# Issuing two sets of small tiled matmuls of neighbouring steps as one alternating run, in a fused recurrence and MLP kernel

## The chip, the cores and the metric

The kernel runs on one core of a Trainium2 chip. The metric is the device time of one execution in microseconds (us); several runs are given by their median. The engines are named as the profile names them: PE (TensorE, the matrix engine; PEld is its weight loads), DVE (VectorE), ACT (ScalarE), POOL (GpSimd) and SP, whose queue issues the loads and stores here. Lines such as L819 are lines of the kernel before.

## The reference

A recurrence over 768 tokens is followed by an MLP. Everything is float32.

```python
# q, k, v: (4, 8, 768, 48), beta: (4, 8, 768)
k_n = k / (norm(k, axis=-1) + 1e-06)
state = zeros((B, H, D, D))
for t in range(S):
    y[:, :, t] = einsum('bhd,bhde->bhe', q[:, :, t], state)
    v_old = einsum('bhde,bhd->bhe', state, k_n[:, :, t])
    state = state + beta[:, :, t, None, None] * einsum('bhd,bhe->bhde', k_n[:, :, t], v[:, :, t] - v_old)
x = y.transpose(0, 2, 1, 3).reshape(B * S, H * D)     # 3072 x 384
h = x @ w_in                                          # 384 x 2048
g = h * clip(h + 3.0, 0.0, 6.0) / 6.0
out = g @ w_out                                       # 2048 x 384
```

## The kernel before

**The recurrence in chunks.** Tokens are taken in 24 steps t of C = 32 tokens. The 128 partitions hold 4 batches of 32 tokens; rows(b) is the stretch of batch b. Inside a chunk the recurrence is solved by a triangular inverse, so a step is a few small matmuls:

- *prep* (L497) makes what does not depend on the state: the scaled keys kb on POOL (L502), transposes pt on PE (L516), KQ on ACT (L524), the products sc of keys and queries on PE (L539), and on DVE the masked L and LB (L550). The mask mb is beta times a triangle of ones, one part positive and one negative (L478, two POOL operations of 128x256 in each step). bkb (L490, POOL) is beta times the keys.
- *inverse* (L738) inverts the triangles of four steps at once on DVE: some sixty operations pr (L751) and A (L756), of growing and then shrinking width, and one transpose back, X (L465, 128x1024). A group's inverse is spread over the steps ahead of the group.
- *chain* (L779) is the part that hangs on the state. ks (L798, 32 matmuls) multiplies the state by keys and queries. R (L892, two DVE operations of 192 columns, and L898, one of 384) combines ks with the values v. pz (L819, 32 matmuls of 32x32 tiles) is X times R, Z (L916, ACT) copies it to SBUF, su (L927, 32 matmuls) is the update of the state and DVE subtracts it (L945, two operations). The output y is made by ACT (L835) and DVE (L811, two operations) from ks, by py = LB times Z (L819, 32 matmuls, of_heads as for pz but with the result in the rows of the neighbouring batch, b ^ 1) and a DVE addition (L854); three PE transposes yt (L864) and an ACT copy (L868) put it into xT, the MLP's input.

pz, py, ph, po and yt share the four banks of the PSUM pool psM; ks, sc and su share the two of psC.

**The MLP in units.** Two steps make a block of 256 tokens. A block's MLP is `up` (ph, L983, then relu on ACT, L991, and g on DVE, L994) and `down` (po, L1145). From block 5 on `up_by_eleven` (L1049, ph at L1055) takes eleven products of half tiles instead of more full ones; it needs sums of the block's tokens, which `token_sums` (L1038) makes with four DVE operations (L1046) in place in xT and in beta_tok, and sums of weights on POOL (L1020). `down_by_seven` (L1190, po at L1210) does the same for the second product: sums of g on DVE (L1196), copies of the products on ACT (L1217), and additions on POOL and DVE (L1220). The last of these are the line u<-u,po on DVE, four POOL additions that hang on it or on each other, and o<-u,po on DVE, which waits for POOL and for the last product. A block is 14 units of down and 16 units of up.

**What sets the order.** Every engine runs its instructions in program order. For the first five steps the order is a string written by hand (ORDER, at the top of the file). From step LS = 5 on a loop (L1434 and below) goes over t and, inside it, over NU = 15 units u. `plan[u]` names the pieces of chain, prep and token sums that are issued ahead of unit u: ks in u = 0, R in 1 and 2, y's first part in 3, pz in 4, Z after it, su and py about u = 8, and the transposes of y at u = 10, and token_sums at u = 11 of odd steps. A generator `fill` supplies pieces of the inverse after each unit. It is paced by `room`, which subtracts from 1.65 us what the unit (USED) and the planned piece (CHAIN) take of DVE, and by `left`, the pieces not issued. At unit 2 of a group's first step, what is left of the inverse is issued at once, X last. `take(ch)` advances the chain to its next yield and `needs` asserts that what it names has been issued.

**Loads.** All go through SP's queue in the order of issue. k, q and v of a step come in four transfers of 48 KB each, one for each batch (L160, L172, L185). v goes into one of two buffers vf; v(t) has to wait until R(t-2) has read its buffer.

Of the kernel before, what the change touches and what calls it, by code (L numbers as in the profile page):

```python
# [9 lines left out]
FP32 = mybir.dt.float32  # L10
# [36 lines left out]
def kernel(  # L47
# [71 lines left out]
    mb_spare = spares[:, 8 * H * C : 10 * H * C]  # L119
# [57 lines left out]
    NVF = 2  # L177

    def load_v(t):
        if t < N:  # L180
            if t >= NVF:
                needs(("R", t - NVF))
            vfs[t] = stage.tile([P, H, D], FP32, name="vf", bufs=NVF)
            for b in range(B):
                nc.sync.dma_start(out=vfs[t][rows(b)], in_=tokens(v, b, t))  # L185
                if b == B - 1:
                    past.add(("v", t))
                yield
# [15 lines left out]
    mask2 = const.tile([P, 2, C], FP32, name="mask2")  # L204
    for j, value in enumerate((1.0, -1.0)):
        m = mask2[:, j, :]
        for b in range(B):
            nc.gpsimd.memset(mask2[rows(b), j, :], value)
            nc.gpsimd.affine_select(
                out=mask2[rows(b), j, :], in_=mask2[rows(b), j, :], pattern=[[1, C]],  # L210
                compare_op=ALU.is_gt, fill=0.0, base=0, channel_multiplier=-1,
            )
# [178 lines left out]
    def norms(g, i0, n):  # L391
# [16 lines left out]
        root = small.tile([P, n, H], FP32, name="root")  # L408
        nc.scalar.activation(out=root[:], in_=ss[:], func=ACTF.Sqrt, bias=tiny, scale=0.25)
        yield  # L410
        t = small.tile([P, n, H], FP32, name="nt")
# [55 lines left out]
    def mask(t):  # L467
# [3 lines left out]
        if early and t % 2 == 0:  # L471
            mb = mb_spare.rearrange("p (e a j w) -> p e a j w", e=2, j=2, w=C)
        else:
            mb = work.tile([P, 2, NP, 2, C], FP32, name="mb", bufs=1)
        mbs[t] = mb
        needs("beta")
        for e in range(2):
            nc.gpsimd.tensor_tensor(  # L478
                out=mb[:, e],
                in0=beta_tok[:, t, e:H:2].unsqueeze(2).unsqueeze(3).to_broadcast([P, NP, 2, C]),  # L480
                in1=mask2[:].unsqueeze(1).to_broadcast([P, NP, 2, C]),
                op=ALU.mult,
            )
# [13 lines left out]
    def prep(t, whole=True):  # L497
# [11 lines left out]
        for j, src in enumerate((kb, qb)):  # L509
# [18 lines left out]
            if whole and j == 0:  # L528
                drain(mask(t))
# [19 lines left out]
        for j, out in enumerate((lowers(t), LB)):  # L549
            nc.vector.tensor_tensor(  # L550
                out=out.rearrange("p (e a) w -> p e a w", e=2), in0=scv[:, :, :, j, :],
                in1=mb[:, :, :, j, :], op=ALU.mult,
# [214 lines left out]
    xTs, outs, zs = {}, {}, {}  # L767
# [11 lines left out]
    def chain(t, whole=True):  # L779
# [45 lines left out]

        def pairs(ph):
            return ph[:, :, 0 : NP * D].rearrange("p e (a w) -> p e a w", w=D)

        def output(Z=None):

            if t > 0:
                needs(("turned", t - 1))
            y = work.tile([P, DM], FP32, name="y", bufs=1)
# [10 lines left out]
            needs(("Z", t))  # L844
            Z = zs.pop(t)
            ring("pm", NPM, ("py", t))
            py = psM.tile([P, 512], FP32, name="py", tag="pm")
            of_heads(py, lambda b: b ^ 1, lambda h: LB[:, he(h), :], Z)
            past.add(("BZ", t))
            yield  # L850
            if t == 0:
                nc.scalar.activation(out=y[:], in_=py[:, 0:DM], func=ACTF.Copy)
            else:
                nc.vector.tensor_tensor(out=y[:], in0=y[:], in1=py[:, 0:DM], op=ALU.add)  # L854
# [28 lines left out]
        if t == 0:  # L883
            R = vfl
        else:
            needs("parity")
            needs(("BZ", t - 1), ("su", t - 1))
            Rt = work.tile([P, DM], FP32, name="R", bufs=1)
            R = Rt[:]
            Rp = R.rearrange("p (e z) -> p e z", e=2)  # L890
            for e in range(2):
                nc.vector.scalar_tensor_tensor(  # L892
                    out=Rp[:, e].rearrange("p (a w) -> p a w", w=D), in0=even[:, e],
                    scalar=parity[:, 0, 0:1], in1=by_pair(vfl)[:, e], op0=ALU.mult, op1=ALU.add,
                )
            if whole:
                yield
            nc.vector.scalar_tensor_tensor(  # L898
                out=Rp, in0=odd.rearrange("p e a w -> p e (a w)"), scalar=parity[:, 1, 0:1],
# [626 lines left out]
```

## Time and profile before

| what | value |
|---|---|
| median of three runs | 678.71 us |
| lowest and highest run | 673.54, 679.48 us |
| the profiled execution, first to last instruction | 673.6 us |
| mean clock granted to PE in it | 0.992 |
| start of ks in steps 5, 9, 13, 17, 21 | 161.8, 267.6, 369.3, 469.9, 565.9 us |
| pz's first matmul after the first of ks, steps 10 to 17 | 7.3 us |
| DVE R L892 (192 columns), L898 (384) | 46 x 404 ns, 23 x 611 ns |
| POOL mb L478 | 38 x 720 ns and 10 x 851 ns |

The page gives each engine's busy time, then the span in forty slices with a busy share in tenths, then the chain of work that ended last, followed back from the last instruction. A row of the timeline is start, duration, engine, line, operation, tiles and number of records; a matmul of float32 leaves two records, so 32 matmuls show as x64. In brackets stand the idle time before and what released it. The profiled execution's time is that of its span, with nothing further known around it; the lowest run lies at the span.

### The profile page before, as it was taken

What the parts mean: (1) busy time and instruction counts of PE and PEld (TensorE: products, weight loads), DVE (VectorE), ACT (ScalarE), POOL (GpSimd) and SP (SyncE); (2) the same over time, 40 slices, a digit from 0 to 9 for tenths busy, and PEclk for the clock granted to TensorE, in tenths of its full rate; (3) what the DMA queues carried; (4) which work ended last, traced back from release to release, by engine and by line L of the source; (5) the groups of instructions that cost most, each with busy time, mean ns of one, the idle gap of its engine ahead of it and who ended that gap; (6) DMA issues with size and microseconds to landing.
All of it is one profiled execution on the core that took longest, in us unless ns stands there. A gap on an engine that the chain in (4) does not pass through costs nothing.

```text
span 673.6 us, 26871 instructions
## 1 busy us (share of the span) xinstructions
PE 636.8 (95%) x11768; PEld 578.6 (86%) x11768; DVE 497.2 (74%) x1226; ACT 271.2 (40%) x532; POOL 206.4 (31%) x320
## 2 busy tenths in 40 slices
PE   2667989999999999999999999999999999999997
PEld 2557877776688988988999999999999999999997
DVE  5978876888545678947888957988748988557354
ACT  5995777422143232232235235245244144153250
POOL 6230231102431031254155255055042141232330
PEclk9989899999999999999999999999999999999999
DMA  7995336402041030032030030020020020010000
GB/s 192 243 218 131 91 78 150 84 1 48 15 82 28 2 72 2 3 70 39 3 64 12 2 67 9 3 61 3 2 49 3 2 49 2 17 23 2 26 1 23
DMA packets 88500, 33.29 MB, mean 49 GB/s; under 512 B 80160, under 2 KB 83232, under 8 KB 88384
## 3 DMA queue, kind: packets, MB, share of 16 engines
q1 hardware_dynamic: 88128, 31.29, 20.9%
q8 instruction: 92, 1.51, 0.9%
q10 hardware_dynamic: 256, 0.30, 0.2%
q14 instruction: 24, 0.20, 0.1%
HBM read 26.84 MB, written 4.72 MB: 47 GB/s over the span
## 4 chain that ended last, share of the span: by engine, by line
PE 86%; DVE 6%; DMA 2%; ACT 2%; issue 2%; SPq 1%; POOL 0%; ACTq 0%; DVEq 0%; POOLq 0%
PE po L1210 27%; PE ph L1055 20%; PE ph L983 15%; PE po L1145 6%; PE ks L798 3%; PE pz L819 3%; PE su L927 3%; PE py L819 3%; PE sc L539 3%; PE pt L516 3%; ACT spare L348 1%; PE yt L864 1%; DVE spare L375 1%; DMA spare<-in_moe_w_in_dram 1%; DMA qb<-in_q_dram 1%
## 5 line engine op out<-in xcount | busy, mean ns | idle before, releaser
L1055 PE MATMUL ph<-xT,w_in 128*128 128x128 f32 x784 | 122.9, 278 | 0.0
L983 PE MATMUL ph<-xT,w_in 128*128 128x256 f32 (+1 forms) x576 | 114.9, 350 | 3.4 <-DVE g L994 2.1
L1210 PE MATMUL po<-w_out,g 128*128 128x192 f32 x640 | 110.6, 326 | 0.0
L983 PEld LDWEIGHTS ph<-xT,w_in 128*128 128x128 f32 x576 | 94.3, 192 | 15.3 <-DVE g L994 2.5
L1055 PEld LDWEIGHTS ph<-xT,w_in 128*128 128x128 f32 x784 | 103.9, 192 | 1.4 <-ACT KQ L524 0.2
L1210 PEld LDWEIGHTS po<-w_out,g 128*128 128x128 f32 x640 | 104.1, 190 | 0.2
L1020 POOL TENSOR_TENSOR g<-g 128x256 f32<-128x256 f32 x112 | 68.1, 610 | 83.9 <-ACT g L1069 79.5
L1210 PE MATMUL po<-spare,g 128*128 128x192 f32 x480 | 86.7, 332 | 0.0
L1210 PEld LDWEIGHTS po<-spare,g 128*128 128x128 f32 x480 | 77.2, 190 | 1.8
L991 ACT ACTIVATE g<-ph,halves 128x256 f32<-128x256 f32 (+1 forms) x96 | 41.2, 436 | 79.1 <-PE ph L983 79.1
L1220 POOL TENSOR_TENSOR o<-o,u 128x192 f32<-128x192 f32 x18 | 15.0, 835 | 172.1 <-ACT o L1217 97.4
L1196 DVE TENSOR_TENSOR g<-g 128x256 f32<-128x256 f32 x160 | 63.4, 443 | 3.4 <-PE po L1210 3.1
L1069 ACT ACTIVATE g<-ph 128x512 f32<-128x512 f32 x56 | 33.4, 596 | 79.9 <-PE ph L1055 76.7
L756 DVE TENSOR_TENSOR A<-A,pr 128x30 f32<-128x30 f32 (+9 forms) x150 | 59.0, 393 | 3.7
L751 DVE TENSOR_TENSOR pr<-A 128x30 f32<-128x30 f32 (+9 forms) x150 | 55.2, 368 | 2.7
L994 DVE SCALAR_TENSOR_TENSOR g<-g,ph 128x256 f32<-128x256 f32 (+1 forms) x96 | 35.0, 370 | 26.0 <-ACT g L991 25.7
L348 ACT ACTIVATE spare<-spare,places 128x768 uint16<-128x768 uint16 (+1 forms) x56 | 52.4, 940 | 2.0 <-DMA spare<-in_moe_w_in_dram 1.1
L1084 DVE TENSOR_TENSOR g<-ph,g 128x256 f32<-128x256 f32 x56 | 23.4, 419 | 38.1 <-PE ph L1055 24.1
L1217 ACT ACTIVATE o<-po 128x192 f32<-128x192 f32 x40 | 13.2, 330 | 82.5 <-PE po L1210 78.9
L1098 DVE SCALAR_TENSOR_TENSOR g<-o,g 128x512 f32<-128x512 f32 x56 | 40.8, 729 | 7.3 <-ACT o L1095 7.3
L1145 PE MATMUL po<-w_out,g 128*128 128x384 f32 x128 | 45.6, 493 | 0.0
L1095 ACT ACTIVATE o<-g,halves 128x512 f32<-128x512 f32 x56 | 40.5, 722 | 11.3 <-DVE g L1098 5.7
(141 smaller groups left out, 991.4 us busy)
## 6 DMA issues: line engine op xcount, KB each, us to landing
kf<-in_k_dram SPq DMA_DIRECT2D x96, 48.0 KB, 2.8
qb<-in_q_dram SPq DMA_DIRECT2D x96, 48.0 KB, 2.9
vf<-in_v_dram SPq DMA_DIRECT2D x96, 48.0 KB, 2.1
out_dram<-o SPq DMA_DIRECT2D x92, 48.0 KB, 1.6
spare<-in_moe_w_in_dram SPq DMA_DIRECT2D x4, 768.0 KB, 6.7
w_out<-in_moe_w_in_dram SPq DMA_DIRECT2D x4, 768.0 KB, 6.0
w_out<-in_moe_w_out_dram SPq DMA_DIRECT2D x4, 768.0 KB, 6.0
spare<-in_moe_w_out_dram SPq DMA_DIRECT2D x4, 768.0 KB, 4.6
```

Of the source, the lines that this page charges most:

```text
L348: nc.scalar.activation(out=z, in_=z if n else d.bitcast(I16)[:, :, :, 3], func=func, bias=places[:, n : n + 1], scale=scale,)
L751: nc.vector.tensor_tensor(out=pv, in0=A[:, j + 1 :, j].unsqueeze(2).to_broadcast([n, w, j]), in1=A[:, j, 0:j].unsqueeze(1).to_broadcast([n ...
L756: nc.vector.tensor_tensor(out=A[:, j + 1 :, 0:j], in0=A[:, j + 1 :, 0:j], in1=pv, op=ALU.subtract)
L983: nc.tensor.matmul(ph[:, cols], lhsT=w_in[:, s, f * 128 : (f + 1) * 128], rhs=xT[:, s, cols], start=(s == 0), stop=(s == NKT - 1),)
L991: nc.scalar.activation(out=g, in_=ph, func=ACTF.Relu, bias=half, scale=1.0 / 6.0)
L1020: nc.gpsimd.tensor_tensor(out=out, in0=a, in1=b, op=op)
L1055: nc.tensor.matmul(ph[:, n], lhsT=w, rhs=x, start=start, stop=stop, skip_group_check=True)
L1095: nc.scalar.activation(out=r, in_=g, func=ACTF.Relu, bias=half, scale=1.0 / 6.0)
L1098: nc.vector.scalar_tensor_tensor(out=g, in0=r, scalar=1.0, in1=g, op0=ALU.min, op1=ALU.mult)
L1145: nc.tensor.matmul(pos[c][:], lhsT=gs[blk, f // 2][:, f % 2, c * P : (c + 1) * P], rhs=w_out[:, f, :], start=(f == 0), stop=(f == NFC - 1),)
L1196: nc.vector.tensor_tensor(out=A(f, *out), in0=A(f, *a), in1=A(f, *b), op=op)
L1210: nc.tensor.matmul(ps[n][:], lhsT=A(f - f % 2, *a)[:, f % 2], rhs=b[:, f], start=(f == 0), stop=(f == HF - 1),)
```

## The change

Four things are done.

1. A new `of_two` issues the matmuls of pz (step t) and py (step t-1) alternately: for each head and batch the tile (b, b) of pz and then the tile (b, b ^ 1) of py, 64 matmuls in one run, in two PSUM banks. It is used when t-1 lies in `late = range(10, 23)`, so for t = 11 to 23. In these steps y(t-1) is finished in step t: its last part is issued at u = 5 and 6, the token sums at u = 8 of the even step instead of u = 11 of the odd one, and u = 10 and 11 hold no piece of the chain. y has two buffers.
2. The mask has one sign and half the size (one POOL operation), and y takes py with a subtraction.
3. R and Z are made in place in the tile that v was loaded into, stored by the parity of the heads. R is two DVE operations of 384 columns. v comes in eight transfers of 24 KB, in three buffers; v(t) has to wait for py and su of t-3. 
4. Steps 7, 8 and 9 have 12 units and step 10 has 13; the units that this leaves come after step 23. JOINED replaces CHAIN in the pacing of the joined steps.

The diff, without the changes of names and the construction of the mask:

```diff
-    NVF = 2
+    NVF = 3
 
     def load_v(t):
         if t < N:
             if t >= NVF:
-                needs(("R", t - NVF))
+                needs(("BZ", t - NVF), ("su", t - NVF))
             vfs[t] = stage.tile([P, H, D], FP32, name="vf", bufs=NVF)
             for b in range(B):
-                nc.sync.dma_start(out=vfs[t][rows(b)], in_=tokens(v, b, t))
+                for e in range(2):
+                    nc.sync.dma_start(
+                        out=vfs[t][rows(b), NP * e : NP * e + NP],
+                        in_=v[b, e::2, t * C : (t + 1) * C, :].rearrange("a t d -> t a d"),
+                    )
                 if b == B - 1:
                     past.add(("v", t))
...
+            mb = work.tile([P, 2, NP, C], FP32, name="mb", bufs=1)
         mbs[t] = mb
         needs("beta")
-        for e in range(2):
-            nc.gpsimd.tensor_tensor(
-                out=mb[:, e],
-                in0=beta_tok[:, t, e:H:2].unsqueeze(2).unsqueeze(3).to_broadcast([P, NP, 2, C]),
-                in1=mask2[:].unsqueeze(1).to_broadcast([P, NP, 2, C]),
-                op=ALU.mult,
-            )
+        nc.gpsimd.tensor_tensor(
+            out=mb[:],
+            in0=beta_tok[:, t, 0:H].rearrange("p (a e) -> p e a", e=2).unsqueeze(3).to_broadcast(
+                [P, 2, NP, C]
+            ),
+            in1=mask[:].unsqueeze(1).unsqueeze(1).to_broadcast([P, 2, NP, C]),
...
+    NYB = 2
+    LATE = 10
+    late = range(LATE, N - 1)
+    xTs, outs, zs, pys = {}, {}, {}, {}
...
+        def of_two(pz, m, z, py, m1, z1):
+            for h in range(H):
+                for b in range(B):
+                    for ps, c, x, y, i in ((pz, b, m, z, he(h)), (py, b ^ 1, m1, z1, h)):
+                        nc.tensor.matmul(
+                            ps[rows(c), D * h : D * h + D],
+                            lhsT=x(h)[rows(b)], rhs=y[rows(b), D * i : D * i + D],
+                            start=True, stop=True, skip_group_check=True,
+                            tile_position=(C * b, C * c),
+                        )
...
-            if t > 0:
-                needs(("turned", t - 1))
-            y = work.tile([P, DM], FP32, name="y", bufs=1)
+            if t > NYB - 1:
+                needs(("turned", t - NYB))
+            y = work.tile([P, DM], FP32, name="y", bufs=NYB)
...
-            needs(("Z", t))
-            Z = zs.pop(t)
-            ring("pm", NPM, ("py", t))
-            py = psM.tile([P, 512], FP32, name="py", tag="pm")
-            of_heads(py, lambda b: b ^ 1, lambda h: LB[:, he(h), :], Z)
-            past.add(("BZ", t))
-            yield
+            if t not in late:
+                needs(("Z", t))
+                Z = zs.pop(t)
+                ring("pm", NPM, ("py", t))
+                py = psM.tile([P, 512], FP32, name="py", tag="pm")
+                of_heads(py, lambda b: b ^ 1, lambda h: LB[:, he(h), :], Z)
+                past.add(("BZ", t))
+                yield
+            else:
+                needs(("BZ", t))
+                py = pys.pop(t)
             if t == 0:
-                nc.scalar.activation(out=y[:], in_=py[:, 0:DM], func=ACTF.Copy)
+                nc.scalar.activation(out=y[:], in_=py[:, 0:DM], func=ACTF.Copy, scale=-1.0)
             else:
-                nc.vector.tensor_tensor(out=y[:], in0=y[:], in1=py[:, 0:DM], op=ALU.add)
+                nc.vector.tensor_tensor(out=y[:], in0=y[:], in1=py[:, 0:DM], op=ALU.subtract)
...
-        if t == 0:
-            R = vfl
-        else:
+        R = vfl
+        if t > 0:
             needs("parity")
-            needs(("BZ", t - 1), ("su", t - 1))
-            Rt = work.tile([P, DM], FP32, name="R", bufs=1)
-            R = Rt[:]
-            Rp = R.rearrange("p (e z) -> p e z", e=2)
-            for e in range(2):
+            Re = R.rearrange("p (e z) -> p e z", e=2)
+            for half, x in ((0, even), (1, odd)):
                 nc.vector.scalar_tensor_tensor(
-                    out=Rp[:, e].rearrange("p (a w) -> p a w", w=D), in0=even[:, e],
-                    scalar=parity[:, 0, 0:1], in1=by_pair(vfl)[:, e], op0=ALU.mult, op1=ALU.add,
+                    out=Re, in0=x.rearrange("p e a w -> p e (a w)"),
+                    scalar=parity[:, half, 0:1], in1=Re, op0=ALU.mult, op1=ALU.add,
                 )
-            if whole:
-                yield
-            nc.vector.scalar_tensor_tensor(
-                out=Rp, in0=odd.rearrange("p e a w -> p e (a w)"), scalar=parity[:, 1, 0:1],
-                in1=Rp, op0=ALU.mult, op1=ALU.add,
-            )
-            yield
+                if whole or half:
+                    yield
...
-        of_heads(pz, lambda b: b, lambda h: X(t)[:, he(h), :], R, he if t else lambda h: h)
+        if t - 1 in late:
+            ring("pm", NPM, ("py", t - 1))
+            pys[t - 1] = psM.tile([P, 512], FP32, name="py", tag="pm")
+            LB1 = LBs[t - 1]
+            of_two(
+                pz, lambda h: X(t)[:, he(h), :], R,
+                pys[t - 1], lambda h: LB1[:, he(h), :], zs.pop(t - 1),
+            )
+            past.add(("BZ", t - 1))
+        else:
+            of_heads(pz, lambda b: b, lambda h: X(t)[:, he(h), :], R, he)
         past.add(("pz", t))
         yield 1
         read(("pz", t))
-        Zt = Rt if t > 0 else work.tile([P, DM], FP32, name="R", bufs=1)
-        nc.scalar.activation(out=Zt[:], in_=pz[:, 0:DM], func=ACTF.Copy)
-        Z = zs[t] = Zt[:]
+        nc.scalar.activation(out=R, in_=pz[:, 0:DM], func=ACTF.Copy)
+        Z = zs[t] = R
         past.add(("Z", t))
         yield
+        if t - 1 in late:
+            for _ in range(2):
+                take(outs[t - 1])
+                yield
...
-        if whole:
+        if whole and t not in late:
...
-    NU = 15
+    UNITS = {7: 12, 8: 12, 9: 12, 10: 13}
...
+        JOINED = {**CHAIN, 5: 0.5, 10: 0.3}
         for t in range(LS, N):
+            NU = UNITS.get(t, 15)
...
+                NU - 2: lambda: take(later),
             }
+            if t - 1 in late:
+                plan[5] = lambda: (take(ch), take(now))
+                plan[6] = lambda: (take(ch), take(now))
+                plan[8] = lambda: (take(ch), t % CB or token_sums(t // CB - 1))
+                if t in late:
+                    del plan[10], plan[11]
...
-                room = max(1.65 - USED[mode["of"]] - CHAIN.get(u, 0), 0.15) / mode["mean"]
+                room = max(1.65 - USED[mode["of"]] - (JOINED if t - 1 in late else CHAIN).get(u, 0), 0.15) / mode["mean"]
```

## The prediction

> **What bounds the kernel now.** I read the page's busy shares first, then its slices, then the chain that ended last, and after that the waits and the timeline of the stretch that the change touches.
>
> ```profile
> span 673.6 us, 26871 instructions
> PE 636.8 (95%) x11768; PEld 578.6 (86%) x11768; DVE 497.2 (74%) x1226; ACT 271.2 (40%) x532; POOL 206.4 (31%) x320
> ...
> PE   2667989999999999999999999999999999999997
> ...
> DVE  5978876888545678947888957988748988557354
> ...
> PE 86%; DVE 6%; DMA 2%; ACT 2%; issue 2%; SPq 1%; POOL 0%; ACTq 0%; DVEq 0%; POOLq 0%
> ```
>
> PE is the bound: 95% busy, 86% of the chain, and full in nearly every slice from the seventh (about 117 us) on. DVE has room on average but not everywhere: its slices stand at 8 and 9 where the down products' sums are made. From 117 us to the end, the waits of PE are these two, 0.9 us in all:
>
> ```profile
> PE pz L819 <- DVE R L898: 0.6, 1, 0.6
> PE pz L819 <- DVE X L465: 0.3, 1, 0.3
> ```
>
> So in this stretch time is won only by less PE work, and any wait that the change puts before PE is paid in full. What one small run costs PE is the distance between starts in its timeline:
>
> ```profile
> 401.48 0.88 PE L819 MATMUL pz<-R,X 32*32 32x48 f32 x64
> 402.29 0.86 PE L539 MATMUL sc<-KQ 64*32 64x64 f32 x64
> 403.08 0.49 PE L1055 MATMUL ph<-xT,w_in 128*128 128x128 f32 x2
> ...
> 408.18 0.89 PE L927 MATMUL su<-R,bkb 32*64 32x48 f32 x64
> 409.00 0.88 PE L819 MATMUL py<-R,LB 32*32 32x48 f32 x64
> 409.81 0.49 PE L1055 MATMUL ph<-xT,w_in 128*128 128x128 f32 x2
> ```
>
> pz takes 0.81 us (32 matmuls, 64 records, four tiles in turn), py 0.81, su 0.82, sc 0.79.
>
> **The change part by part.**
>
> *A. The joined run (t = 11 to 23, 13 of them).* It removes 13 x (0.81 + 0.81) and adds 13 runs of 64 matmuls over eight tiles. Before has one run of that size, the double sc of a whole prep:
>
> ```profile
> 115.46 1.48 PE L539 MATMUL sc<-KQ 64*32 64x64 f32 x128
> 116.87 0.91 PE L1145 MATMUL po<-w_out,g 128*128 128x384 f32 x2
> ```
>
> 64 matmuls over eight tiles in 1.41 us. I take that for the joined run: 13 x (1.62 - 1.41) = **-2.7 us**. Upper end of the gain: in the raw records of sc and su the first 32 come 6.7 ns apart and only the rest at about 10; if all 128 came at 6.7 ns the run would be about 1.0 us, -8 us. Lower end: two tiles that share a row group (pz at (b,b), py at (b,b^1)) do not overlap at all; then only one of two entries and exits is saved (0.13 by the difference between the 0.68 us from first to last pz record and the 0.81), -1.7 us.
> A rule of the Trainium skill speaks against the change here: TensorE: Matmul & The Clock Gate, Part 3, What overlaps and what doesn't, has a weight load overlap the matmuls in flight only when its row group differs. By that rule the second tile of each pair would load behind the first, and the alternation would be worse than two runs that go round four row groups: an estimate of 2.7 us a run, +14 us in all (rival 3 has its working). The rows above disagree: sc and su have two tiles in each row group as well, and cost no more than pz.
>
> *B. Steps 7 to 9 have 12 units and step 10 has 13, not 15.* The work moves to the tail (11 units), PE work unchanged: 0. But the inverse of the group that begins with step 9 has less time. Its DVE operations (pr, A) drain ahead of X in the first units of step 9. Before, ks(9) starts at 267.63, X runs 273.24 to 275.22, pz at 275.37, already 0.38 late. By the changed order seven pairs instead of four stand between step 9's beginning and X. The three that come in (168, 150, 130 wide) took 265.98 to 268.03 = 2.05 us before. Step 9 then also begins in an up stretch, where DVE stands behind g, which waits for ACT (an interval of 1.0 us between g at 242.87 and 243.90). X would end 9.6 to 11.0 us behind ks, with pz wanted at 7.3: a wait of 2.3 to 3.8, less the 0.38 of before. Ends +1.7 and +4.5; I take **+3.5**, since the row of the up stretch is the nearer one.
>
> *C1. R as two operations of 384 elements* (0.61 each) instead of two of 192 and one of 384 (0.40, 0.40, 0.61): DVE -0.2 us a step. y becomes a subtraction, same size. Both lie beside PE: 0.
> *C2. Step 21.* Its way from ks to pz is short (565.85 to 572.33) and X(21) ends at 570.29 only; R's halves follow (0.61, two g of 0.33, 0.61), so R is done about 6.2 to 6.5 behind ks, where PE arrives at 6.2: **+0.5** (0 to 1.5).
>
> *C3. The token sums of blocks 5 to 10 (steps 12, 14, ... 22).* This is the largest term. y(t-1) is now finished in step t, so its sums stand at unit 8 of step t. In the changed order they stand on DVE behind the last output add, o<-u,po, where they stood ahead of it; and su now stands on PE between the last down products and the first ph of the new block. Before:
>
> ```profile
> 388.19 0.35 DVE L1220 TENSOR_TENSOR u<-u,po 128x192 f32<-128x192 f32 x1 [0.74 <-PE po L1210]
> ...
> 389.04 0.39 DVE L1046 TENSOR_TENSOR beta_tok<-xT 128x128 f32<-128x128 f32 x1 [0.40 <-ACT xT L868]
> ...
> 390.61 0.28 DVE L1046 TENSOR_TENSOR beta_tok<-xT,beta_tok 128x128 f32<-128x128 f32 x1
> 391.38 0.35 DVE L1220 TENSOR_TENSOR o<-u,po 128x192 f32<-128x192 f32 x1 [0.48 <-POOL o L1220]
> ```
>
> o waits for POOL's four adds (388.68 to 391.34, 2.66 us), so it ends at 391.73. DVE runs its program in order: pr and A steps (0 to 0.7) and the sums are queued behind it, and they take 1.85 us from first to last. PE's first ph needs only xT, the second the first sum, the third the sum that is ready 1.4 to 1.65 behind. In these coordinates ph begins 0.82 (su) later than the 390.92 of before, 391.74, and wants the third matmul at 392.18, two steps of 0.22 on. It gets its operand at 391.73 + 1.4 to 2.35 = 393.1 to 394.1: 0.9 to 1.9 us late. By each block's own operations before the sums, the six come to 1.7, 1.4, 1.8, 1.3, 1.8, 0.9, that is **+8.9 us** (7 to 11; 0 if something takes the sums ahead of o after all). What is late next is g of that unit, hidden behind the ph that follow.
>
> *D. Values.* v comes in 8 transfers of 24 KB a step instead of 4 of 48. SP takes 0.45 to 0.5 us for each (k's two at 83.25 took 0.94). In the first 60 us that is 12 more, about 5.9 us of SP time, in front of q, k and the weights in that queue; q and k loads behind them are issued later too. Against it, SP waits less: v's buffer (three instead of two) made it stand 13.5 us (two waits, before 83 us) for R. **0**, ends -3 and +3. The price of the other wait: v(t) now waits for su(t-3), three steps back, long done.
> *E. mask* is one POOL operation of 256 instead of two (0.72 to 0.85 each), the norms have one buffer, y two. POOL is at 31%: 0, unless POOL's adds of C3 come sooner by it, which is within the 7 of that range.
>
> **Sum:** -2.7 + 3.5 + 0.5 + 8.9 = +10.2 us on the profiled 673.6, 683.8. That execution agrees with the lowest of the runs shown (673.54); the median is 678.71, with one run at 679.48 beside it. 678.7 + 10.2 = 688.9, which I put at **688**, since a PE that waits lets DVE catch up for what follows.
>
> **The rivals.**
> 1. *The sums cost nothing* (0.21). POOL's or DVE's place moves so that o is done earlier, by the smaller mask for one. Then A + B + C2 = +1.3: 680. For it: POOL is free there, and idle 4.25 us before its first add; against it: the four adds depend on u, which depends on PE's second last po.
> 2. *The other side: the joined run goes at the rate of the first 32 records* (0.08). Its place is PE L836, its price 13 x (1.62 - 1.0) = -8, and it decides only if C3 is at most about 1 us as well: 678.7 - 8 + 1 = 671 or 672. For it: the 6.7 ns between records is seen in every run; against it: double sc, 1.41, the only run of that length.
> 3. *Tiles of one row group hold each other up* (0.09). In pz's records a tile comes round every 0.0425 us. If the two records of each pair stand that far apart, the joined run takes 64 x 0.0425 = 2.7 us, and A is 13 x (2.7 - 1.62) = +14 where I have -2.7: 705. For it: in sc and su the tiles of one row group come in another turn than here; against it: those runs cost no more than pz.
> 4. *SP at the start* (0.05). If the 5.9 us of issues reach the weights, ACT's conversions of the last pieces, which the trace has landed about 3 us before ACT takes them, start 5.9 - 3 = 2.9 us later: +3 on the forecast, 692.
>
> **How the numbers follow.** My forecast has 0.57. The likeliest case alone: 684 to 693 (C3 7 to 11, B 1.7 to 4.5, A -1.7 to -5.4, with part of each cancelling). The range takes in rival 1 and 4 and reaches towards 3 and 2: 676 to 698. A measurement of this kernel can tell about 1% (6.8 us) from no change. Faster by over 1% is rival 2: 0.08. Within 1% (672 to 685.5): rival 1 and the low edge of the forecast, 0.21 + 0.07 = 0.28. Slower: the rest, 0.64.
>
> **What would show it.** A: starts around the joined run 1.41 apart (1.0: rival 2; 2.4: rival 3). B: one wait of about 3.8 us of PE at the run of step 9, released by DVE X. C3: PE's ph waiting for DVE beta_tok or xT, six times, 0.9 to 1.9 us, near the ends of the down stretches. C2: a wait of half a microsecond for R in step 21. D: the start of ks(5) within 3 us of 161.85. I am wrong if PE's waits from 117 us on sum to less than 5 us, or if the pz that starts a run waits at other steps, for v say.

## The result and the profile after

The changed kernel takes 695.69 us (median of 4 runs, 694.7 to 698.17) against 678.31 (4 runs, 673.54 to 679.48) for the kernel before: a ratio of 1.0284, 95% interval 1.0244 to 1.0323, slower by 17.4 us at the medians. The profiled executions differ by 20.1 us, 673.6 and 693.7. In each run since, the device time lies 1.7 to 1.8 us above the span. So the execution that was profiled before, with its span of 673.6, will have taken some 675.3 us (an estimate from these runs) and was not the lowest run of 673.54. The sum on the profiled time is that much too low; the 688 goes by the median and is not touched.

The page of the changed kernel:

```profile
span 693.7 us, 27017 instructions
...
PE 643.7 (93%) x11768; PEld 583.3 (84%) x11768; DVE 486.1 (70%) x1203; ACT 271.6 (39%) x532; POOL 183.7 (26%) x288
...
PE   2678989999999997999999998999999998998997
...
PE 81%; DVE 11%; issue 3%; ACT 2%; DMA 1%; POOL 1%; SPq 0%; DVEq 0%; ACTq 0%; POOLq 0%
```

PE is still the bound, but the row of nines has gaps, and DVE has 11% of the chain where it had 6. DVE and POOL are less busy than before (486.1 for 497.2, 183.7 for 206.4), which bought nothing. The waits of PE from 117 us on (time in all, times, longest):

```profile
PE pz L825 <- DVE X L467: 3.6, 1, 3.6
PE yt L885 <- DVE y L875: 2.8, 2, 2.3
PE sc L542 <- issue: 2.0, 1, 2.0
PE pz L836 <- DVE vf L909: 1.9, 2, 1.2
PE ph L1080 <- ACT vf L937: 1.7, 3, 0.6
PE ph L1080 <- DVE beta_tok L1071: 1.3, 3, 0.5
PE pz L836 <- ACT o L1242: 0.8, 1, 0.8
PE po L1235 <- issue: 0.6, 1, 0.6
```

14.7 us, where the kernel before had 0.9. No single wait is large: there are 14 in eight kinds. In six kinds PE arrives early at a result of the new order; in the two marked issue it waits for nothing that the profile shows. The first and the third row have a second part. The timeline of step 9 and the stretches around it (us of the stretch, busy time of PE, PEld, DVE, ACT, POOL, then the granted clock):

```profile
270.79 1.91 DVE L467 STREAM_TRANSPOSE X<-A 128x1024 f32<-128x1024 f32 x1
```

```profile
272.80:274.00 1.20, 1.15 (x60) 1.19 (x64) 1.20 (x5) 0.00 (x0) 0.00 (x0) 0.50 0.00 0
274.00:276.00 2.00, 2.00 (x85) 1.71 (x75) 0.68 (x3) 0.49 (x1) 0.00 (x0) 0.50 0.04 8
...
280.00:284.00 4.00, 4.00 (x144) 3.66 (x143) 3.01 (x7) 0.44 (x2) 1.91 (x2) 1.00 0.00 0
```

X ends at 272.70, pz starts at 272.85, and PE then runs at half clock until 278.3: "busy" for 5.5 us and doing the work of 2.7. Such time hides in the busy time of PE, which is up by 6.9 us at an equal number of instructions; the waits do not show it. Behind the stop inside sc of step 15 it is the same: ph's records come 0.214 us apart instead of 0.112 from 425.2 to 428.4.

The joined run itself, and that stop:

```profile
420.38 0.23 PE L836 MATMUL pz<-vf,X 32*32 32x48 f32 x1
...
421.68 0.54 PE L542 MATMUL sc<-KQ 64*32 64x64 f32 x34
424.21 0.45 PE L542 MATMUL sc<-KQ 64*32 64x64 f32 x30 [1.99 <-issue]
```

From the first matmul of the joined run to sc are 1.30 us; two runs took 1.62. That gain is real, 13 x 0.32 = 4.2 us.

To leave the start aside, where executions of either kernel differ by some us, the experiments are compared by the time from ks of step 5 to the end of the profiled span: 511.8 us before (673.6 - 161.8), 529.9 after (693.7 - 163.8), so 18.1 us more. From the gaps between starts on PE: X in step 9 +3.3 (3.7 less 0.4 before) and its half clock +2.6; the stop in sc +2.2 and its half clock +1.6; the token sums +3.3; the last parts of y +3.1; R in steps 16 and 21 +2.0, less the 0.6 that R of step 18 cost before; ph behind Z +1.9; a pz behind ACT's o +0.9; a po +0.7; the joined run -4.2. That is 16.8; 1.3 us are not assigned.

### The profile page after: what moved, and what is told of

Same layout as the page of the kernel before. It is cut to its first block, busy times and chain, and to the rows that moved or that the text cites. A ratio compares the mean times of both kernels' runs of the same rounds, so it can differ in the third digit from the quotient of the medians.

```text
span 693.7 us, 27017 instructions
## 1 busy us (share of the span) xinstructions
PE 643.7 (93%) x11768; PEld 583.3 (84%) x11768; DVE 486.1 (70%) x1203; ACT 271.6 (39%) x532; POOL 183.7 (26%) x288
## 3 DMA queue, kind: packets, MB, share of 16 engines
q8 instruction: 92, 1.51, 0.9%
## 4 chain that ended last, share of the span: by engine, by line
PE 81%; DVE 11%; issue 3%; ACT 2%; DMA 1%; POOL 1%; SPq 0%; DVEq 0%; ACTq 0%; POOLq 0%
PE po L1235 22%; PE ph L1080 20%; PE ph L1008 15%; PE po L1170 6%; PE ks L804 3%; PE pt L519 3%; PE sc L542 2%; PE su L952 2%; DVE pr L754 1%; DVE A L759 1%; PE py L825 1%; DVE g L1221 1%; PE pz L836 1%; PE pz L825 1%; PE yt L885 1%
## 5 line engine op out<-in xcount | busy, mean ns | idle before, releaser
L1080 PE MATMUL ph<-xT,w_in 128*128 128x128 f32 x784 | 124.9, 281 | 2.3 <-ACT vf L937 1.7
L1008 PE MATMUL ph<-xT,w_in 128*128 128x256 f32 (+1 forms) x576 | 116.7, 355 | 1.1 <-ACT spare L350 1.1
L1235 PE MATMUL po<-w_out,g 128*128 128x192 f32 x640 | 112.8, 329 | 0.0
L1080 PEld LDWEIGHTS ph<-xT,w_in 128*128 128x128 f32 x784 | 104.7, 193 | 4.9 <-ACT vf L937 2.1
L1008 PEld LDWEIGHTS ph<-xT,w_in 128*128 128x128 f32 x576 | 95.7, 196 | 12.6 <-issue 1.0
L1235 PEld LDWEIGHTS po<-w_out,g 128*128 128x128 f32 x640 | 105.5, 192 | 0.5 <-issue 0.2
L1245 POOL TENSOR_TENSOR o<-o,u 128x192 f32<-128x192 f32 x18 | 12.8, 712 | 175.6 <-ACT o L1242 85.6
L754 DVE TENSOR_TENSOR pr<-A 128x30 f32<-128x30 f32 (+9 forms) x150 | 57.2, 381 | 2.6
L1080 PE MATMUL ph<-beta_tok,sums_in 128*128 128x128 f32 x224 | 44.1, 279 | 1.3 <-DVE beta_tok L1071 1.3
```

Of the source, the lines that this page charges most:

```text
L754: nc.vector.tensor_tensor(out=pv, in0=A[:, j + 1 :, j].unsqueeze(2).to_broadcast([n, w, j]), in1=A[:, j, 0:j].unsqueeze(1).to_broadcast([n ...
L1008: nc.tensor.matmul(ph[:, cols], lhsT=w_in[:, s, f * 128 : (f + 1) * 128], rhs=xT[:, s, cols], start=(s == 0), stop=(s == NKT - 1),)
L1080: nc.tensor.matmul(ph[:, n], lhsT=w, rhs=x, start=start, stop=stop, skip_group_check=True)
L1235: nc.tensor.matmul(ps[n][:], lhsT=A(f - f % 2, *a)[:, f % 2], rhs=b[:, f], start=(f == 0), stop=(f == HF - 1),)
```

## The experiments

Each is the changed kernel with the edit shown, if nothing else is said. Ratios are to the kernel before, run beside each. A time from ks of step 5 is that of one profile; set against the changed kernel's, it agrees within 2 us with what the ratios say, in experiment 12 within 4.

**1. The inverse ends in step 8.**

```diff
-    room = max(1.65 - USED[mode["of"]] - ...
-    due += room * left / max((GS - i) * NU - u, 1)
-    due = min(due, 2.6)
+    room = max((2.4 if t < 9 else 1.65) - USED[mode["of"]] - ...
+    due += room * left / max((GS - i) * NU - u - (4 if t < 9 else 0), 1)
+    due = min(due, 3.2 if t < 9 else 2.6)
```

> The changed kernel with one edit: the inverse of the group that begins with step 9 is paced so that it ends in step 8. Theory (a late X stops PE for 3.62 us in step 9, and the stop brings the half clock that the profile shows from 272.85 to 278.1, about 2.6 us more): the stop goes and the half clock with it, the profiled span falls by about 6 us, from 693.7 to 688. Rival 1 (the half clock there is not brought by the stop): the span falls by 3.6 and the half clock stays. Rival 2 (DVE has no room in steps 7 and 8): the stop moves into steps 7 and 8 and the span does not fall.

Measured: ratio 1.0218 [1.0168, 1.0268], 526.8 us from ks of step 5. The stop in step 9 and its half clock went, but PE now stopped in step 8:

```profile
249.97 3.35 PE L1008 MATMUL ph<-xT,w_in 128*128 128x256 f32 x7 [2.58 <-DVE g L1019]
```

and ran at half clock from 250 to 253. A miss for the expected 6 us: 3.0 were gained. Rival 2 holds as far as the stop moved, since DVE had no room left in those shorter steps, but it had expected no gain.

**2. The units taken from elsewhere.**

```diff
-    UNITS = {7: 12, 8: 12, 9: 12, 10: 13}
+    UNITS = {8: 13, 9: 11, 10: 10}
-    room = max(1.65 - ...
+    room = max((2.0 if t < 9 else 1.65) - ...
```

> The changed kernel with one part set otherwise: the 11 units are taken from steps 8, 9 and 10 (2, 4 and 5 units fewer) instead of 7 to 10, and the inverse before step 9 is paced a little faster (2.0 for 1.65), so that two pairs of pr and A instead of seven stand behind R of step 9. Theory (the stop of 3.6 us in step 9 and the half clock behind it belong to where the units were taken): the wait for X in step 9 is under 1 us, no half clock follows, and from ks of step 5 on the kernel takes 524 instead of 529.9 us. Rival (DVE has no room for it, as in the run that ended the inverse in step 8, which got 2.8 us of new waits in step 8): other waits of DVE in steps 8 to 10 make up for it and less than 2 us are gained.

Measured: ratio 1.0193 [1.0146, 1.024], 523.8 us from ks of step 5 (524 expected). There is no wait for X and no half clock around step 9, and none came elsewhere. So the choice of the shortened steps, with the pace of the inverse before step 9, cost 6.1 us, stop and half clock together.

**3. The token sums ahead of the output add.**

```diff
-    plan[8] = lambda: (take(ch), t % CB or token_sums(t // CB - 1))
+    plan[7] = lambda: t % CB or token_sums(t // CB - 1)
+    plan[8] = lambda: take(ch)
```

> The changed kernel with one edit: the token sums of the joined steps are issued at unit 7, on DVE ahead of the last output add instead of behind it. My forecast priced their place at 8.9 us. The profile after shows only about 3.3 us of it (gaps of ph behind beta_tok and xT in six blocks, 0.6 us the longest). Theory (as the profile shows): the span falls by about 3 us and those gaps go. Rival (the forecast's price, the rest being hidden in other waits): it falls by 7 to 9 us. Second rival: ahead of the add the sums run beside POOL's adds and are slow again (0.4 to 0.67 us each as in the kernel before, 0.28 in the changed one), so that part of the wait comes back and the gain is 1 us or less.

Measured: ratio 1.0211 [1.0163, 1.026], 524.9 us from ks of step 5, 5.0 less; the gaps of ph behind the sums are gone. Each of the two profiles has two half clocks, the second at another place, so the 1.7 us beyond the 3.3 of the gaps can't be given to the sums. The sums themselves, first in the changed kernel, then in this one:

```profile
403.70 0.35 DVE L1245 TENSOR_TENSOR o<-u,po 128x192 f32<-128x192 f32 x1 [2.65 <-POOL o L1245]
...
404.32 0.28 DVE L1071 TENSOR_TENSOR beta_tok<-xT 128x128 f32<-128x128 f32 x1
...
404.85 0.29 DVE L1071 TENSOR_TENSOR xT<-xT 128x128 f32<-128x128 f32 x1
```

```profile
402.40 0.45 DVE L1071 TENSOR_TENSOR beta_tok<-xT 128x128 f32<-128x128 f32 x1 [0.43 <-ACT xT L889]
402.89 0.64 DVE L1071 TENSOR_TENSOR beta_tok<-xT,beta_tok 128x128 f32<-128x128 f32 x1
403.45 0.67 DVE L1071 TENSOR_TENSOR xT<-xT 128x128 f32<-128x128 f32 x1
404.05 0.28 DVE L1071 TENSOR_TENSOR beta_tok<-xT,beta_tok 128x128 f32<-128x128 f32 x1
404.05 0.72 POOL L1245 TENSOR_TENSOR o<-o 128x192 f32<-128x192 f32 x1
```

Behind the add they take 0.28 us each; ahead of it three of the four take 0.45 to 0.67, beside POOL's four adds, which run from 402.12 to 404.77 there. The fourth starts together with POOL's last add and keeps its 0.28; that add takes 0.72 us, where POOL's four take 0.59 each in the changed kernel. The second rival's premise is right, its conclusion wrong: the sums are slow again and still early enough, as PE wants them only at 405.52.

**4. Two runs in the place of the alternating one.**

```diff
-    of_two(pz, lambda h: X(t)[:, he(h), :], R, pys[t - 1], lambda h: LB1[:, he(h), :], zs.pop(t - 1))
+    of_heads(pz, lambda b: b, lambda h: X(t)[:, he(h), :], R, he)
+    of_heads(pys[t - 1], lambda b: b ^ 1, lambda h: LB1[:, he(h), :], zs.pop(t - 1))
```

> The changed kernel with one edit: pz and py stand in the same place, but as two runs one behind the other, 32 matmuls of pz and then 32 of py, not alternately. Theory: one run costs 1.30 us and two cost 1.62, so the span rises by 13 x 0.32 = 4.2 us. Rival 1 (alternation itself is worth nothing, only the shared entry and exit): two runs cost 1.49, +2.5 us. Rival 2 (the PE stop of 2.0 us inside sc in step 15, with the half clock behind it, comes from the alternating run using up PE's instructions faster than they are loaded): the stop goes, 3.6 us are won back and the span is nearly unchanged.

Measured: ratio 1.0283 [1.0233, 1.0333], 531.1 us from ks of step 5, only 1.2 more.

```profile
524.03 0.88 PE L825 MATMUL pz<-vf,X 32*32 32x48 f32 x64
524.72 0.88 PE L825 MATMUL py<-vf,LB 32*32 32x48 f32 x64
525.53 0.49 PE L1078 MATMUL ph<-xT,w_in 128*128 128x128 f32 x2
```

Neighbouring runs cost 0.69 + 0.81 = 1.50 where ph follows and 1.47 where sc or po does: standing side by side is worth 0.12 to 0.15 of the 0.32, alternation 0.17 to 0.20, 2.2 to 2.6 us in 13 steps (rival 1's 1.49). But the three waits of ph for Z are gone: Z's copy starts 0.95 us behind the run's first matmul, and 1.39 in the alternating one (which starts at 523.31), where pz is ready only with py. The copy here, then in the changed kernel:

```profile
524.98 0.49 ACT L935 ACTIVATE vf<-pz 128x384 f32<-128x384 f32 x1 [0.42 <-PE pz L825]
```

```profile
524.70 0.49 ACT L937 ACTIVATE vf<-pz 128x384 f32<-128x384 f32 x1 [0.86 <-PE py L836]
```

This profile also has a half clock behind the last y, which the changed kernel's has not, so the 1.2 us are not the alternation's alone. The stop inside sc stayed (1.54 us), so rival 2 falls: alternation did not bring it.

**5. v in four transfers.**

```diff
-    for e in range(2):
-        nc.sync.dma_start(out=vfs[t][rows(b), NP * e : NP * e + NP], in_=v[b, e::2, ...])
+    nc.sync.dma_start(out=vfs[t][rows(b)], in_=tokens(v, b, t))
```

> The changed kernel with one edit: v comes in four transfers of 48 KB a step instead of eight of 24 KB, in the natural order of the heads, so the values are given to the wrong heads (the output is another one; the work and its sizes are the same). Theory (SP's queue is longer at the start by 12 transfers of 0.49 us): ks of step 5 starts about 2 us earlier, at 162 instead of 163.8, and the span falls by 2. Rival (the 2 us are a matter of the clock steps in the first 90 us, which fall differently in each execution): no change beyond 1 us that holds over the rounds.

Measured: ratio 1.0235 [1.0203, 1.0267]. ks of step 5 starts at 162.3. That is 1.5 of the 2 us expected, but nothing follows from it: with eight transfers it lies between 159.8 and 166.9 in the other profiles, and in two profiles of edited kernels before, with four, at 164.8 and 163.7. From there on this kernel takes 528.6. The start shows no cost of the loads that can be told from its own spread, and the intervals of the two kernels' ratios overlap.

**6. sc apart from the joined run.**

```diff
+    plan[4] = lambda: take(ch)
     plan[5] = lambda: (take(ch), take(now))
     plan[6] = lambda: (take(ch), take(now))
+    plan[7] = lambda: take(now)
```

> The changed kernel with one edit: in the joined steps sc is issued one unit later, no longer directly behind the joined run, and what follows it one unit later too. In all five profiles with the changed order PE stopped 1.5 to 2.0 us inside sc of step 15 and waited for nothing that the profile shows, also when pz and py were two runs; before, where 32 matmuls stood ahead of sc and not 64, it never did. Theory (so many small matmuls in one row use up the loaded instructions before the next block of 16 KB has come; in that profile such a block was on its way at 421.6 to 422.9): apart, the stop goes, and where a half clock followed it, that too; 2 to 3.6 us less from ks of step 5 on. Rival (it hangs on where the block's end falls in the program and not on the row of small matmuls): a stop of the same length stays at that place or comes at another.

Measured: ratio 1.0273 [1.0235, 1.0312], 529.9 us from ks of step 5, no gain. The stop in sc went (0.3 us is left in another step), and its half clock too; in their place ph waits for Z in three more steps, 0.56 each, since sc had stood between the joined run and the ph that needs a bank, and ph waits 2.1 instead of 1.3 us for the sums. So the theory is half right: apart, the stop goes, and the waits that sc had covered take its place.
In the changed kernel's profile an instruction block of 16 KB was on its way from 421.6 to 422.9 when PE stopped at 422.0. In all six profiles with 64 + 32 small matmuls in a row PE stopped there for 1.5 to 2.0 us; in the four with sc apart in that step it did so for 0, 0, 0.3 and 0.8 us. But the same row stands in six other steps of the changed kernel (11 to 14, 16 and 17), and there PE did not stop, so the row is not enough: the place in the program counts too, as the rival had it. And the stops on issue go with these blocks. From 117 us on the profiles of all runs have 18 of over 0.15 us (without the one in step 9 of experiment 5, which stands where X is late), and each ended 1.3 to 1.6 us after a block of 16 KB had landed; in the changed kernel such blocks come 3.6 to 10.4 us apart from 300 to 480 us. That the loading of instructions falls behind at the end of a block, and most behind a row of small matmuls, fits all this; no run shows which instruction PE lacked, so it stays a reading.

**7 and 8. Stops put into the kernel before,** in six steps, by a chain of POOL operations between R and pz (44 memsets, then 18).

```diff
+        if t in range(12, 24, 2):
+            idle = work.tile([P, 32], FP32, name="idle", bufs=1)
+            nc.gpsimd.tensor_tensor(out=idle[:, 0:1], in0=R[:, 0:1], in1=R[:, 0:1], op=ALU.subtract)
+            for _ in range(44):
+                nc.gpsimd.memset(idle[:, 1:32], 1.0)
+            nc.gpsimd.tensor_tensor(out=R[:, 0:1], in0=R[:, 0:1], in1=idle[:, 1:2], op=ALU.mult)
```

> The kernel before, with a chain of 46 small POOL operations (44 of them memsets of a tile of its own) between R and pz in steps 12, 14, 16, 18, 20 and 22; nothing else is changed. At 0.1 to 0.12 us each the chain is 4.5 to 5.5 us long against the 3.2 us between R's end and pz in the profile before, so PE should stop six times for 1.5 to 2.3 us. Theory (a stop of this size brings the half clock at some of its places, not at all, and the half clock costs up to 2.6 us): the span rises by more than the sum of the stops, and the granted clock shows 0.5 behind some of the six. Rival (the half clock has nothing to do with the stops): the clock stays 1.0 from 117 us on, and the span rises by just their sum, 9 to 14 us.

> As in stops, with 18 memsets instead of 44. There the chain of 46 operations stopped PE for 8.76 us behind 3.2 us of cover, 0.26 us an operation; 20 operations make 5.2 us, six stops of 2.0 us, the length of the one in sc of step 15 that was followed by a half clock in the profile after and not in two others. The long stops cost 15.2 us more than their 52.6 us from ks of step 5 on, 2.5 each, with the clock at 0.5 behind all six. Theory (a short stop brings the half clock at some of its places only): one to five of the six are followed by 0.5, and the kernel takes 12 us plus 1.5 to 2.6 for each of those from ks of step 5 on. Rival (only stops of over 3 us bring it): none is, and it takes 12 us more, 524.

Measured: ratios 1.1005 [1.0969, 1.1041] and 1.0513 [1.0468, 1.0558]. Both chains came out longer than meant: six stops of 8.8 us (52.6 in all) and of 4.0 to 4.3 (24.6). In the traces the 46 operations take 8.33 us and the 20 take 3.59, 0.18 each, and they begin 0.6 to 1.8 us behind R, when POOL has done its own additions of g; the 0.26 of the second expectation holds this delay too. From ks of step 5 on the kernels take 579.6 and 547.0, which is 67.8 and 35.2 more than 511.8, so 15.2 and 10.6 beyond the stops: 2.5 and 1.8 us for each. All twelve were followed by half clock; of one of the long ones, from 477.6 to 486.4:

```profile
480.00:484.00 4.00, 0.00 (x0) 0.00 (x0) 0.77 (x3) 0.00 (x0) 2.73 (x23) 0.64 0.00 0
...
486.30:488.00 1.70, 1.63 (x80) 1.51 (x88) 0.00 (x0) 0.01 (x1) 0.02 (x1) 0.50 0.05 10
488.00:490.00 2.00, 2.00 (x69) 1.83 (x59) 0.76 (x2) 0.48 (x1) 0.00 (x0) 0.50 0.00 0
```

The clock falls inside the stop and comes back 5.0 us after PE has work again (4.7 to 6.2 in the six). So the half clock does follow a stop. The question of the 2-us stop was missed by these two, but the other profiles answer it, below.

**9. The rest without the joining.**

```diff
-    LATE = 10
+    LATE = N - 1
-    UNITS = {7: 12, 8: 12, 9: 12, 10: 13}
+    UNITS = {}
```

> The changed kernel without its first part: no step is joined (late is empty) and all steps have 15 units; what stays is the one-signed mask, R and Z in the values' tile with R in two operations, v in eight transfers and three buffers, two buffers of y. Theory (all that costs time comes with the joined steps and the delay of y): within 1% of the kernel before, and from ks of step 5 to the end within 2 us of its 511.8. Rival (the values' loads or R's new form cost time by themselves): over 5 us more, with waits of PE for vf or late starts of ks in steps 1 to 5 that come back in it.

Measured: ratio 0.9988 [0.997, 1.0005], 10 runs against 19, and 512.4 us from ks of step 5.

```profile
PE py L825 <- issue: 0.8, 1, 0.8
PE pz L825 <- DVE X L467: 0.3, 1, 0.3
...
```

The mask, R and Z in place and the loads change nothing that can be measured, though by the page they take 5 us of busy time from DVE (492.6 for 497.2) and 19 from POOL (187.8 for 206.4). All the loss comes with the joining, the delay of y and the shortened steps.

**10. Mended:** experiments 2, 3 and 6 together, and in the last step the transposes of y one unit later.

> The changed kernel with four things mended together: the units taken from steps 8 to 10 and the faster pace (as in units_moved), the token sums ahead of the last output add, sc one unit behind the joined run, and in the last step the transposes of y one unit later and the sums after them. Theory (the loss is the sum of these waits and of the half clock behind two of them: 3.6 + 2.6, 3.3, 2.0 + 1.6, 2.3): from ks of step 5 on 514 to 517 us instead of 529.9, level with the 511.8 of the kernel before, since the joined run's 4.2 us go to its own waits for Z and for ACT. Rival (the waits hide one another, and where one goes the next comes): more than 521 us.

Measured: ratio 1.0119 [1.0082, 1.0155], 518.9 us from ks of step 5, 11.0 less than the changed kernel, and 2 to 5 more than expected.

```profile
PE ph L1080 <- ACT vf L937: 3.4, 6, 0.6
PE pz L836 <- DVE vf L909: 1.9, 2, 1.2
PE yt L885 <- DVE y L875: 1.4, 2, 1.0
...
```

The waits for X and for the sums are gone, the one for the last y is shorter; those for Z have doubled with sc apart, and now are the largest.

**11. Mended, with two runs** (the edit of experiment 4).

> The mended kernel, with pz and py as two runs one behind the other instead of alternately. Theory (the alternation saves 0.32 us in each of 13 steps, 4.2 in all, but Z's copy starts only when both are done, and six waits of ph for it, 0.56 each, 3.4 in all, eat that): from ks of step 5 on 518 to 521 us against the mended kernel's 518.9, and no wait of ph for Z. Rival (those waits come from py's bank and not from Z's late start): they stay, and it takes 523.

Measured: ratio 1.0101 [1.0064, 1.0138], 516.2 us from ks of step 5, below the 518 to 521 expected. The waits for Z are gone:

```profile
PE pz L825 <- DVE vf L909: 1.9, 2, 1.2
PE yt L885 <- DVE y L875: 1.3, 2, 1.0
...
```

Its profile has no half clock behind the start, the mended one has one of about 1.5 us; without that they stand at 516.2 and 517.4. The ratios of the two do not differ beyond their intervals. The alternation, the point of the change, gains nothing that can be seen in this kernel: what it saves on PE's array it returns in waits for Z.

**12. Mended further:** sc apart in step 15 alone, the inverse before step 21 paced at 2.0, the last transposes one more unit later.

> The mended kernel, mended further: sc stands apart from the joined run in step 15 alone, the inverse before step 21 is paced faster (2.0 for 1.65 in steps 18 to 20), and the last transposes of y come one more unit later. Theory (each wait is separate): without three waits for Z less two of 0.56, the wait for R of step 21 (1.2, with the half clock behind it 1.5) and 1.0 for the last y, from ks of step 5 on 514 us instead of 518.9, and the time within 1% of the kernel before. Rival (DVE has no more room there): new waits of DVE in steps 18 to 20, no gain over 2 us.

Measured: ratio 1.0034 [1.0011, 1.0058] (10 runs against 19), 516.8 us from ks of step 5. The gain over the mended kernel is 2.1 us in place of 4.9. The wait for R of step 21 went, but, as the rival had it, R of step 19 became 1.22 us late, and a half clock followed it. The kernel is within 1% of the kernel before and still behind it. No version with the joining beats the kernel before.

## Why the prediction was right, and where its steps were not

The direction, the bound and the range held: the measured 695.7 lies within 676 to 698, 7.7 above the 688 named, and above the 684 to 693 that it called the likeliest case. PE was full, and what came before it was paid in full. But the agreement of the sum hides errors of both signs, and of the prediction's two signs of being wrong one came: PE's waits sum to 14.7 us, not to less than 5, but pz also waited in two other steps, for R in step 16 (0.7 us) and behind ACT's o in step 20 (0.8).

- **A, the joined run** (-2.7): the term was mis-sized, the mechanism right. It takes 1.30 us, not 1.41, so -4.2, between the bounds given. Double sc has four tiles in each row group, where the joined run has two, and stood for the joined run well enough. What the step lacked is that a run of 1.30 us hands over pz 0.44 us later than pz alone, and that this is paid again (+1.9).
The Trainium skill's rule that was weighed against it (TensorE: Matmul & The Clock Gate, Part 3, What overlaps and what doesn't) asked for more than two runs cost; 1.30 against 1.47 to 1.50 for the same matmuls not alternated decides against that estimate.
- **B, step 9** (+3.5): +3.3 by the same late X, right, though its ends of +1.7 and +4.5 do not follow from its own wait of 2.3 to 3.8 less 0.38 (1.9 to 3.4). The step stopped there, as if a wait cost its length; the half clock behind it added 2.6.
- **C1, D, E** (0): right, by experiments 5 and 9.
- **C2, step 21** (+0.5): 1.2 at that place, inside the range given; the same kind of wait came in step 16 (0.7), which was not seen.
- **C3, the token sums** (+8.9): the step that failed in size, 3.3 by the gaps. Place and cause were right, PE's second and third matmul wait for the sums. Their length was copied from rows where POOL worked beside them (0.39 to 0.67 us for three of the four, 1.85 from first to last), into a place where, by the very argument of the step, POOL has just finished. There they take 0.28 each, 1.0 in all.
- **Not in the sum at all**, 13 us: the half clock (2.6 + 1.6), the stop inside sc (2.2), the last parts of y (3.1), ph behind Z (1.9), a pz behind ACT's o (0.9), a po (0.7). Each comes from work that the change moved to another place, and the sum followed only three of the moves.
- **The rivals** did not come: the joined run is neither at 1.0 nor at 2.7 us, SP's queue cost nothing that can be told, and the sums cost 3.3, neither 0 nor 8.9.

C3 was 5.6 us too high and A 1.5 short of its gain, and 13 us were not seen: what made the sum come near was an error that went the other way. That the total came inside the range is in good part luck.

## What to carry to other kernels

Where PE is full, a later use of a result does not cost its own instructions but the slack of everything that hangs on it: here y one step later asked for 11 MLP units of distance, shorter steps, and a new place for each piece, and a dozen small waits came of it. A saving that delays the first of two results (alternating two sets of matmuls) should be set against who waits for that first result. And a duration is copied only together with what ran beside it: a row measured beside a busy POOL is no price for a place where POOL rests.

## What the runs showed of the hardware

**A stop of PE costs more than its length, and how much hangs on where it falls.** Between 117 us and the last stretch, the clock in the profiles shows 0.5 only behind a stop. Counted over all profiles but those of experiments 7 and 8: the stop of 3.6 us was followed by it in five of five, that of 2.6 in the one there is, those of 1.5 to 2.0 in sc in four of six, those of 2.3 at the last y in one of seven, those of 1.2 before R in three of ten, each of these three with another wait of 0.56 us close behind. The same stop (R of step 21, 1.2 us) was followed by it in two profiles and not in seven.

The clock records of the traces explain most of this. In each of the 14 profiles the clock changes only at points that lie whole multiples of 3.41 us apart, and where these points fall differs from execution to execution. Cut at these points from 120 us on, the stretches at full clock in which PE idled 1.9 us or more were all followed by the half clock (21 of 21), those with 1.39 to 1.74 in 5 of 11, and no other. So a stop counts in full where it falls into one stretch, and less where a point divides it. The half clock lasted one or two stretches, 3.4 or 6.8 us (three behind the stops of 8.8 us), in part inside the stop itself, and cost 1.5 to 2.6 us beyond the stop where that was worked out.
The Trainium skill (TensorE: Matmul & The Clock Gate, Part 1, What's actually happening and HAM oscillation) has the rule of thumb that idle gaps of PE over about 3.4 us are to be avoided, by a free-running window. The window agrees with the points found here; the length does not, as 1.9 us of idle in one stretch were always enough here.

**PE can stop inside a run of small matmuls, waiting for nothing that the profile shows.** With 64 + 32 of them in a row it did so at the same place of the program in six profiles of six, for 1.5 to 2.0 us. With 64 in a row (su and py, experiment 9) it did so once, for 0.8 us. The trace has instructions loaded by one queue in 92 transfers of 16 KB, some 1 us each. That they are PE's is an estimate: the queue carries 1.51 of 1.71 MB of instructions, and PE has 23536 of the 27017 in the profile. Experiment 6 has what ties the stops to these transfers.

**DVE's additions of two SBUF tiles are mostly slower beside POOL's:** 128x128 took 0.28 us alone and, in three of four, 0.45 to 0.69 while POOL added, with the order of the two engines' work as the only difference (experiment 3). The fourth started together with a POOL addition and kept its 0.28, and the POOL addition took 0.72 us in the place of 0.59.
The Trainium skill (SBUF — State Buffer, Who interferes with whom) says that a DVE instruction with two SBUF inputs contends with a GpSimd instruction that reads SBUF; this case agrees, and by these rows either side can be the one that pays.
